# Half-height matmuls on two halves of the array, and weight fetches at spaced times, in a fused attention and mixer kernel

## The chip, the cores and the metric

The kernel runs on one core of one Trainium2 chip. The metric is the device time of one execution in microseconds (us). Most executions of one kernel agree within 0.3%. A core has TensorE (PE, matrix multiplication), VectorE (DVE), ScalarE (ACT), GpSimd (POOL) and SyncE (SP, which here issues all DMAs), each with its own instruction queue that is worked off in order.

## The reference

Batch 4, 8 heads, 576 tokens, head size 64, so a model width of 512. Three stages follow each other:

```python
# 1. attention in a window of 32 (heads 0-3) or 32 dilated by 4 (heads 4-7)
attn = softmax(where(mask, q @ k.T / 8, -1e9)); x = attn @ v            # [4, 576, 512]
# 2. channel mix with token shift
xk, xr = mu_k * x + (1 - mu_k) * x_prev, mu_r * x + (1 - mu_r) * x_prev
x = sigmoid(xr @ w_r) * (relu(xk @ w_k) ** 2 @ w_v)                     # 512 -> 1024 -> 512
# 3. mixer
h = relu(x.T @ w_tok1) @ w_tok2; u = x + h.T                            # 576 -> 256 -> 576 tokens
out = u + relu(u @ w_ch1) @ w_ch2                                       # 512 -> 1536 -> 512
```

All arrays are float32 (weights arrive as 64-bit words and are converted on the core).

## The kernel before

Every large product is made of three matmuls (`mm3`): each operand is split into a high and a low float32r part, and high x high, high x low and low x high are added up in a PSUM bank. A high part is a copy, a low part is the value less the high part (`split`).

The function `tile_model` writes the whole computation down in program order, but nothing is emitted in that order. Each operation goes to a `Plan`, which records its reads and writes and from them its dependencies. `Plan.order` then gives each operation a due time and simulates the five engines: whenever an engine is free, it takes, of the operations that are ready, the one with the smallest due time. What an engine executes is this order. For a matmul the due time begins as the sum of the planned costs of all matmuls ahead of it in the program (`at`); it becomes smaller where something that depends on it is due early:

```python
pad = 0 if first[i] == "tensor" else 1.0
due[i] = min(due[i], due[s] - cost[i] - self.TAIL[first[i]] - self.DELAY[first[i]][first[s]] - pad)
```

`slowly` marks conversions of the channel weights that may be put off: `floor` holds their due times back, and an operation listed there isn't ready before its place `at`.

The stages that the change touches:

**Token mix.** The result of stage 2 lies as 18 tiles of 128 tokens x 512 channels, nine for two batches together: four of batch 0, four of batch 1, and a ninth whose upper 64 rows are the last tokens of batch 0 and whose lower 64 rows are the last tokens of batch 1. `tokens_in(b)` multiplies the four tiles of a batch and the shared one by the first token weights (`t1`, two halves m of 128 hidden units) into two PSUM banks, then rectifies the sums (ACT writes the high part, DVE the remainder) into `hid[b]`. For the shared tile `t1` has two pairs, `t1[4]` with zeros in its lower half and `t1[5]` with zeros in its upper half, so all its matmuls take 128 rows; `ends` keeps the tile's split for the second batch. `turn(t)` transposes a tile into `u`, four PE transposes and their copies. `tokens_out(b)` multiplies `hid[b]` by the second token weights (48 matmuls of 288 columns) in turning banks and adds to `u`. In the trace the first product's matmuls show as `bank<-z,at` (whole tiles), `bank<-wr,at` (shared tile with `t1[4]`, batches 0 and 2) and `bank<-wr,z` (shared tile with `t1[5]`, batches 1 and 3), 512 columns each; those of `tokens_out` as `bank<-at,z`, 288 columns; transposes as `bank<-cst,x`.

**Channel mix.** Both products are done with seven products of half-size blocks in place of eight (names A11, S1, A12, S2, S4, S3, A22), in three column chunks c. The first, `middle(c, j)`, 42 matmuls of 384 columns for each of six j, writes its output through two buffers in turn to DRAM (`kept_mid`, in the trace `part_mid<-at`). The second, `result(c)`, 252 matmuls of 384 columns, loads these back and multiplies by `w2`: seven sweeps, one for each name, 36 matmuls each. The operands of `w2`, seven sets of 6 x 2 x 256 words for each partition, lie in DRAM (`kept_w`, in the trace `part_A..` and `part_S..`) and are fetched into places that the first product's weights `w1` hold until the last `middle` calls; a fetch may be issued as soon as its place is free.

**Attention's last step.** `weigh` multiplies 96 rows x 64 columns, alternately into the upper and lower 64 output partitions, in bursts that the planner keeps together (`burst`). Each float32 matmul shows as two instructions (`bank<-x,at 96*64`). The change doesn't touch it.

Of the kernel before, what the change touches and what calls it, by code (L numbers as in the profile page):

```python
# [10 lines left out]
F32R = mybir.dt.float32r  # L11
# [3 lines left out]
AF = mybir.ActivationFunctionType  # L15
# [134 lines left out]
class Plan:  # L150
# [22 lines left out]
    def __init__(self, nc):  # L173
        self.nc = nc
        self.ops, self.deps, self.ages = [], [], []
        self.state, self.early, self.bursts, self.floor = {}, {}, [], {}
        for name in self.ENGINES:
            setattr(self, name, Plan._Engine(self, name))

# [67 lines left out]
    @staticmethod  # L247
    def _cost(engine, method, kw):

        out = kw["out"]  # L250
        cols = int(np.prod(out.shape[1:]))
        pointers = sum(hasattr(kw.get(k), "space") for k in ("scale", "bias", "scalar", "scalar1"))
        if engine == "sync":
            if kw["in_"].dtype == U32:
                return max(0.45, 4 * cols * out.shape[0] / 230e3 - 0.9)
            return max(0.45, 8 * (0.03 + 4 * cols * 0.0266e-3))
        if engine == "tensor":
            if method == "transpose":
                return cols / 1200 + 0.0025
            if kw["lhsT"].dtype in (F32R, BF16):  # L260
                return cols / 2263 + 0.0049
            if kw["lhsT"].shape[0] <= D or out.shape[0] <= D:
                return cols / 1200 + 0.0025
            return 2 * max(cols / 1200 + 0.0025, 0.112)
        source = kw.get("in_", kw.get("in0"))
        psum = source is not None and "PSUM" in str(source.space)
        if engine == "scalar":
            read = 0.093 * (kw.get("accum_out") is not None)
            return (0.07 if psum else 0.1) + cols / 1200 + 0.03 * pointers + read
        if engine == "gpsimd":  # L270
            return 0.04 if method == "memset" else 0.04 + cols / 345
        if method == "tensor_reduce":
            return 0.066 + int(np.prod(source.shape[1:])) / 960
        if method == "reciprocal":
            return 0.066 + cols / 157
        fast = method in ("tensor_copy", "tensor_scalar", "tensor_scalar_add") and not psum
        return 0.066 + 0.05 * pointers + cols / (1920 if fast else 960)
# [16 lines left out]
    def order(self):  # L294
# [23 lines left out]
            for k, i in enumerate(group[1:]):  # L318
                due[i] = -1e6 + k
        left = [len(d) for d in self.deps]  # L320
        ready = [dict.fromkeys(op, at[i] if i in self.floor else 0.0) for i, op in enumerate(self.ops)]
        known = {e: [] for e in self.ENGINES}
        avail = {e: [] for e in self.ENGINES}
        free = dict.fromkeys(self.ENGINES, 0.6)
# [100 lines left out]
def tile_model(nc, banks, kept_1, kept_w, kept_u, kept_mid, units, cst, mu, w_k, w_v, w_r, w_t1, w_t2, w_c1, w_c2, outT):  # L425
    memory = {k: [Slot(f"{k}{i}", n) for i, n in enumerate(v)] for k, v in SLOTS.items()}

    def f(view):
        return view.bitcast(F32)

    def at(place, shape, dtype=F32):
        name, number, offset = place
        return memory[name][number].view(offset, shape, dtype)
# [6 lines left out]
    def cut(name, numbers, size, count=None):  # L440

        out = []
        for n in numbers:
            out += [(name, n, size * i) for i in range(SLOTS[name][n] // size)]
        return out[:count]
# [7 lines left out]
    def mm3(out, lh, ll, rh, rl, first, last, goes_on=False):  # L453

        more = dict(skip_group_check=True) if goes_on else {}
        nc.tensor.matmul(out=out, lhsT=lh, rhs=rh, start=first, stop=False, **more)
        nc.tensor.matmul(out=out, lhsT=lh, rhs=rl, start=False, stop=False, **more)
        nc.tensor.matmul(out=out, lhsT=ll, rhs=rh, start=False, stop=last, **more)
# [10 lines left out]
    def split(raw, hi, lo):  # L469
        copy(hi, raw)  # L470
        combine(lo, raw, f(hi), ALU.subtract)

    def rows(n):
        return slice(128 * n, 128 * n + 128)
# [6 lines left out]
    def pair(place, shape):  # L481

        name, number, offset = place
        n = int(np.prod(shape))
        return at(place, shape, F32R), at((name, number, offset + n), shape, F32R)
# [11 lines left out]

        return words(w).rearrange("(k p) c -> p k c", p=128)[:, :, 2 * n * m:2 * n * m + 2 * n]

    def single(srcs, t, raw_ring, zero=None):  # L500

        n = t.shape[1]
        flat = raw_ring.tile(2 * n, dtype=U32)
        for part, src in srcs:
            dst = flat[part]
            if len(src.shape) == 3:
                dst = dst.split(src.shape[1], src.shape[2])
            nc.sync.dma_start(out=dst, in_=src)
            if raw_ring is raw_a:
                nc.early[len(nc.ops) - 1] = 6  # L510
        if zero is not None:
            nc.gpsimd.memset(out=f(flat[zero]), constant=0.0)
        raw = flat.split(n, 2)
        low, h = raw[:, :, 0], raw[:, :, 1]
        b, half = t.bitcast(U32), t.bitcast(U16)
        v = nc.vector
        nc.scalar.activation(out=t, in_=f(h), func=AF.Prelu, scale=2.0 ** -112, alpha=-(2.0 ** 32))
        v.tensor_scalar(out=b, in0=b, scalar1=3, scalar2=None, op0=ALU.logical_shift_left)
        v.scalar_tensor_tensor(
            out=half, in0=low, scalar=2.0 ** -29, in1=half, op0=ALU.mult, op1=ALU.add  # L520
        )

    def weight(srcs, hi, lo, raw_ring, tmp_ring, zero=None):

        shape = tuple(hi.shape[1:])
        t = tmp_ring.tile(int(np.prod(shape)))
        single(srcs, t, raw_ring, zero)
        split(t.split(*shape) if len(shape) == 2 else t, hi, lo)

    everything = slice(0, 128)  # L530
# [263 lines left out]
    def slowly(convert, *args):  # L794
        start = len(nc.ops)
        convert(*args)
        nc.floor.update(dict.fromkeys(range(start, len(nc.ops)), SLACK))

    nchunk = len(CHUNKS)
    p_ring = psum(5, 6, 7)  # L800
# [37 lines left out]

    t1 = [pair(p, (HID,)) for p in cut("at", (1, 2), 512) + [("at", 0, 4 * S), ("at", 0, 4 * S + 512), z512[8]]]
    t2 = [pair(p, (S,)) for p in cut("at", (0,), 2 * S, 2)]
    xt512 = cut("xt", (2, 0, 1), 512)
    raw_b, tmp_b = ring(xt512[8:10]), ring(xt512[10:12])
# [1 line left out]
        weight([(everything, words(w_t1)[rows(k), :])], *t1[k], raw_b, tmp_b)  # L846
    tail = words(w_t1)[512:576, :]
    halves = [slice(0, 64), slice(64, 128)]
    for odd in range(2):
        weight([(halves[odd], tail)], *t1[4 + odd], raw_b, tmp_b, zero=halves[1 - odd])  # L850
    for k in range(2):
        for n in range(3):
            cs = slice(192 * n, 192 * n + 192)
# [8 lines left out]

    def u(b, kt, cs):
        return whole[kt // 2][:, kt % 2, S * b:S * b + S][:, cs]

    def tiles_of(b):
        base, odd = 9 * (b // 2), b % 2
        return [(base + 4 * odd + i, i) for i in range(4)] + [(base + 8, 4 + odd)]

    spots = cut("wk", range(4), 512) + cut("xt", (2, 0), 512) + cut("wr", (2,), 512) + cut("x2", (5, 6, 0, 1, 2, 3), 512)  # L870
    w1 = []
# [13 lines left out]

    for j in range(3):
        fetch_1(j)
    hid, ends = {}, {}
    hp_r, x2p_r, up_r = psum(0, 1, 2, 3), psum(4, 5), psum(6, 7)
    late_r = psum(6, 7, 4, 5)  # L890

    def tokens_in(b):
        hp = [hp_r.tile(C) for _ in range(2)]
        for n, (t, kt) in enumerate(tiles_of(b)):
            if n < 4:
                h, l = x2h_r.tile(C, dtype=F32R), x2l_r.tile(C, dtype=F32R)
            elif b % 2 == 0:
                h, l = ends[b // 2] = at(("wr", 3, 0), (C,), F32R), at(("wr", 3, 512), (C,), F32R)
            else:
                h, l = ends[b // 2]  # L900
            if n < 4 or b % 2 == 0:
                split(x2[t], h, l)
            for m in range(2):
                mm3(hp[m], t1[kt][0][:, rows(m)], t1[kt][1][:, rows(m)], h, l, n == 0, n == 4)
        hid[b] = []
        for m in range(2):
            h, l = (hid_r.tile(C, dtype=F32R) for _ in range(2))
            nc.scalar.activation(out=h, in_=hp[m], func=AF.Relu)
            nc.vector.scalar_tensor_tensor(
                out=l, in0=hp[m], scalar=0.0, in1=f(h), op0=ALU.max, op1=ALU.subtract  # L910
            )
            hid[b].append((h, l))

    def turn(t):
        tp = x2p_r.tile(4, 128)
# [13 lines left out]
    def tokens_out(b):  # L929
        for kt in range(4):  # L930
            for n in range(2):
                cs = slice(HALF * n, HALF * n + HALF)
                hp = (up_r if b < 2 else late_r).tile(HALF)
                for k in range(2):
                    h, l = hid[b][k]
                    mm3(hp, h[:, rows(kt)], l[:, rows(kt)], t2[k][0][:, cs], t2[k][1][:, cs], k == 0, k == 1)
                nc.vector.tensor_tensor(out=u(b, kt, cs), in0=hp, in1=u(b, kt, cs), op=ALU.add)
# [5 lines left out]
    for t in range(4, 8):  # L943
        turn(t)
    tokens_in(1)
    tokens_out(0)
    for t in range(9, 13):
        turn(t)
    tokens_in(2)
    turn(17)  # L950
    tokens_out(1)
    for t in range(13, 17):
        turn(t)
    tokens_in(3)
    tokens_out(2)
    tokens_out(3)

# [81 lines left out]
        cut("x2", (1, 2, 3), 512)[2:], cut("wr", (0, 1, 3), 512),  # L1039
    ]  # L1040
    w2 = {}
    for name, places in zip(NAMES, w2_at):
        w2[name] = [tuple(at(p, (2, 256), F32R)[:, i] for i in range(2)) for p in places]
        fetch(places, kept_w[name])

    size = 3 * N2
    half_r = ring(
# [180 lines left out]
```

## Time and profile before

| | |
|---|---|
| time, median of 3 runs (lowest to highest) | 675.2 us (674.82 to 675.28) |
| time of the profiled execution | 676.94 us |
| its span, first to last instruction | 675.2 us |
| PE busy, matmuls | 659.4 us |
| DVE / ACT busy | 547.1 / 332.8 us |
| granted TensorE clock, mean | 1.00 |
| moved by DMA | 138.06 MB, mean 204 GB/s |

A busy engine counts from the first to the last instruction in flight; matmuls overlap, so the step from one start to the next is shorter than one matmul's duration. Times in the rows are us from the span's start.

### The profile page before, as it was taken

The numbers are of one execution on the slowest core, as the hardware profiler recorded it, in microseconds if no ns is written. First come the engines' busy times: TensorE is split into PE (matmuls) and PEld (weight loads), VectorE is DVE, ScalarE is ACT, GpSimd is POOL, SyncE is SP. The second block draws the span as 40 slices with busy tenths as digits, with TensorE's granted clock in tenths as the row PEclk, the third lists the DMA queues.
The fourth block names the chain that finished last, engine by engine and source line by source line (L and its number), as shares of the span: only waits on it lengthen the run. The fifth ranks groups of instructions, "written<-read, shape, count | busy, mean of one in ns | idle before, by whom it ended". The sixth has DMA issues, their size and how long they took to land.

```text
span 675.2 us, 11417 instructions
## 1 busy us (share of the span) xinstructions
PE 659.4 (98%) x4153; PEld 609.8 (90%) x4153; DVE 547.1 (81%) x1127; ACT 332.8 (49%) x886; POOL 2.1 (0%) x22
## 2 busy tenths in 40 slices
PE   6899999999999999999999999999998999999997
PEld 6677888888898888888878999999998999999997
DVE  4899998799689799598877659788695769998982
ACT  4989874578476467375542236563171122212310
POOL 0000000000000000000000000000000000000000
PEclk9999999999999999999999999999999999999999
DMA  8988343556656234428871356947788899632211
GB/s 315 380 318 328 108 145 108 182 160 202 189 169 193 86 138 164 160 79 313 303 252 63 95 205 240 332 174 271 249 298 334 261 390 402 219 94 93 71 36 60
DMA packets 61064, 138.06 MB, mean 204 GB/s; under 512 B 5328, under 2 KB 24656, under 8 KB 59984
## 3 DMA queue, kind: packets, MB, share of 16 engines
q1 hardware_dynamic: 61008, 137.33, 59.4%
q8 instruction: 33, 0.54, 0.3%
q14 instruction: 23, 0.19, 0.1%
HBM read 91.70 MB, written 45.61 MB: 203 GB/s over the span
## 4 chain that ended last, share of the span: by engine, by line
PE 86%; DMA 7%; DVE 3%; ACT 2%; issue 1%; SPq 0%; DVEq 0%; ACTq 0%
PE bank L411 86%; DMA x<-w_k 2%; DMA part_mid<-at 1%; DMA wr<-units 1%; ACT z L411 1%; DVE z L411 1%; DMA wv<-units 1%; DMA raw<-w_v 1%; ACT x L411 1%; DMA xt<-w_t 1%; DVE at L411 1%; DVE xt L411 0%; ACT at L411 0%; SPq L411 0%; DVE x L411 0%
## 5 line engine op out<-in xcount | busy, mean ns | idle before, releaser
L411 PE MATMUL bank<-z,wk 128*128 128x384 f32 x800 | 180.0, 343 | 1.9 <-DVE at L411 1.7
L411 PEld LDWEIGHTS bank<-z,wk 128*128 128x128 f32 x800 | 141.0, 188 | 9.3 <-DVE at L411 2.0
L411 PE MATMUL bank<-wv,z 128*128 128x512 f32 x432 | 129.4, 403 | 0.4 <-ACT z L411 0.4
L411 PEld LDWEIGHTS bank<-wv,z 128*128 128x128 f32 x432 | 78.0, 188 | 12.7 <-ACT z L411 0.8
L411 ACT ACTIVATE at<-at 128x96 f32<-128x96 f32 (+2 forms) x177 | 64.3, 365 | 24.3 <-DVE at L411 22.9
L411 PE MATMUL bank<-wr,z 128*128 128x512 f32 x228 | 62.8, 402 | 1.2 <-DVE z L411 1.2
L411 ACT ACTIVATE z<-bank 128x384 f32<-128x384 f32 (+2 forms) x60 | 29.7, 498 | 52.9 <-PE bank L411 52.6
L411 DVE TENSOR_TENSOR z<-z,z 128x384 fp32r<-128x384 f32 (+1 forms) x94 | 53.0, 569 | 3.1 <-ACT z L411 2.0
L411 PE MATMUL bank<-xt,wk 128*128 128x384 f32 x254 | 53.9, 345 | 1.3 <-ACT at L411 1.3
L411 PEld LDWEIGHTS bank<-wr,z 128*128 128x128 f32 x228 | 41.4, 188 | 8.8 <-DVE z L411 1.6
L411 DVE SCALAR_TENSOR_TENSOR z<-bank,z 128x384 f32<-128x384 f32 (+1 forms) x56 | 31.9, 573 | 21.1 <-ACT z L411 21.1
L411 PE MATMUL bank<-xt,x 128*128 128x384 f32 x248 | 48.8, 334 | 0.0
L411 PE MATMUL bank<-z,x 128*128 128x384 f32 x232 | 47.0, 334 | 0.0
L411 PEld LDWEIGHTS bank<-xt,wk 128*128 128x128 f32 x254 | 44.5, 188 | 2.5 <-issue 1.5
L411 DVE TENSOR_TENSOR at<-bank,at 128x384 f32<-128x384 f32 x64 | 35.3, 552 | 10.7 <-PE bank L411 10.4
L411 PEld LDWEIGHTS bank<-xt,x 128*128 128x128 f32 x248 | 43.5, 188 | 0.0
L411 ACT ACTIVATE z<-z 128x384 fp32r<-128x384 f32 x69 | 35.4, 523 | 11.3 <-DVE z L411 10.0
L411 PEld LDWEIGHTS bank<-z,x 128*128 128x128 f32 x232 | 40.8, 188 | 0.0
L411 ACT ACTIVATE at<-bank 128x384 f32<-128x384 f32 x35 | 17.1, 489 | 38.5 <-PE bank L411 37.6
L411 ACT ACTIVATE x<-bank 96x512 f32<-96x512 f32 (+1 forms) x48 | 28.1, 589 | 14.6 <-PE bank L411 14.3
L411 DVE SCALAR_TENSOR_TENSOR z<-xt,cst,z 128x256 f32<-128x256 f32 (+3 forms) x92 | 34.1, 404 | 0.8 <-ACT z L411 0.4
L411 ACT ACTIVATE z<-xt,cst 128x256 f32<-128x256 f32 (+3 forms) x65 | 26.6, 443 | 10.3 <-DVE z L411 9.9
(170 smaller groups left out, 1164.1 us busy)
## 6 DMA issues: line engine op xcount, KB each, us to landing
part_mid<-at SPq DMA_DIRECT2D x18, 768.0 KB, 5.0
z<-part_mid SPq DMA_DIRECT2D x11, 576.0 KB, 8.0
x<-w_c SPq DMA_DIRECT2D x12, 512.0 KB, 4.0
at<-units SPq DMA_DIRECT2D x14, 416.0 KB, 4.1
unit<-units SPq DMA_DIRECT2D x13, 416.0 KB, 4.4
at<-units SPq DMA_DIRECT2D x21, 256.0 KB, 4.1
part_w<-wv SPq DMA_DIRECT2D x21, 256.0 KB, 3.2
part_w<-x SPq DMA_DIRECT2D x21, 256.0 KB, 3.0
```

Of the source, the lines that this page charges most:

```text
L411: call(kw["out"], kw["constant"]) if method == "memset" else call(**kw)
```

## The change

The fetch of each set of `w2` gets an earliest planned time: the place of the fetches in the plan, plus 5 us for each set ahead of it, less 2 us (`hold`). `floor` and `hold` are told apart: the conversions marked by `slowly` keep both.

The shared tile is no longer padded with zeros. `t1` has one pair for it, whose upper half serves the even batch and whose lower half the odd one. `tokens_in(b)` ends with the four whole tiles, and a new `tokens_end(g)` adds the shared tile for both batches of a group: 64-row matmuls, the even batch on partitions 0 to 63, the odd one on 64 to 127, written down in alternation; then it rectifies all four sums. The planner prices such a matmul at half. Transposes 9 to 12 move ahead of `tokens_out(0)`.

```diff
@@ Plan._cost
             if kw["lhsT"].dtype in (F32R, BF16):
-                return cols / 2263 + 0.0049
+                return (cols / 2263 + 0.0049) * (0.5 if kw["lhsT"].shape[0] <= D else 1)
@@ Plan.order
-        ready = [dict.fromkeys(op, at[i] if i in self.floor else 0.0) for i, op in enumerate(self.ops)]
+        ready = [dict.fromkeys(op, at[i] + self.hold[i] if i in self.hold else 0.0) for i, op in enumerate(self.ops)]
@@ slowly
         nc.floor.update(dict.fromkeys(range(start, len(nc.ops)), SLACK))
+        nc.hold.update(dict.fromkeys(range(start, len(nc.ops)), 0.0))
@@ tile_model, token weights
-    t1 = [pair(p, (HID,)) for p in cut("at", (1, 2), 512) + [("at", 0, 4 * S), ("at", 0, 4 * S + 512), z512[8]]]
+    t1 = [pair(p, (HID,)) for p in cut("at", (1, 2), 512) + [("at", 0, 4 * S), ("at", 0, 4 * S + 512)]]
...
-    for odd in range(2):
-        weight([(halves[odd], tail)], *t1[4 + odd], raw_b, tmp_b, zero=halves[1 - odd])
+    weight([(half, tail) for half in halves], *t1[4], raw_b, tmp_b)
@@ token mix
+    def tokens_end(g):
+        h, l = at(("wr", 3, 0), (C,), F32R), at(("wr", 3, 512), (C,), F32R)
+        split(x2[9 * g + 8], h, l)
+        both = list(zip((2 * g, 2 * g + 1), halves))
         for m in range(2):
...
+            high, low = (w[:, rows(m)] for w in t1[4])
+            for left, right, last in (high, h, False), (high, l, False), (low, h, True):
+                for b, half in both:
+                    nc.tensor.matmul(out=sums_of[b][m], lhsT=left[half], rhs=right[half], start=False, stop=last)
+        for b, _ in both:
+            hid[b] = []
+            for m in range(2):
+                h, l = (hid_r.tile(C, dtype=F32R) for _ in range(2))
+                nc.scalar.activation(out=h, in_=sums_of[b][m], func=AF.Relu)
+                nc.vector.scalar_tensor_tensor(
+                    out=l, in0=sums_of[b][m], scalar=0.0, in1=f(h), op0=ALU.max, op1=ALU.subtract
+                )
+                hid[b].append((h, l))
@@ order of the token mix
     tokens_in(1)
-    tokens_out(0)
+    tokens_end(0)
     for t in range(9, 13):
         turn(t)
+    tokens_out(0)
     tokens_in(2)
     turn(17)
     tokens_out(1)
     for t in range(13, 17):
         turn(t)
     tokens_in(3)
+    tokens_end(1)
     tokens_out(2)
     tokens_out(3)
@@ fetches of w2
-    for name, places in zip(NAMES, w2_at):
+    for n, (name, places) in enumerate(zip(NAMES, w2_at)):
+        start = len(nc.ops)
         w2[name] = [tuple(at(p, (2, 256), F32R)[:, i] for i in range(2)) for p in places]
         fetch(places, kept_w[name])
+        nc.hold.update(dict.fromkeys(range(start, len(nc.ops)), 5.0 * n - 2.0))
```

## Rows read from the trace of the kernel before

**Rows 1.** The page, part 1: busy us, share of the span, instructions

```profile
PE 659.4 (98%) x4153; PEld 609.8 (90%) x4153; DVE 547.1 (81%) x1127; ACT 332.8 (49%) x886; POOL 2.1 (0%) x22
```

**Rows 2.** The chain that ended last, its last part: start us, us, what

```profile
500.07 9.56 DMA part_mid<-at
...
511.23 160.45 PE bank L411 x924
```

**Rows 3.** Timeline of SP's queue, VectorE and PE around 505: start us, us, what

```profile
499.12 0.32 SPq L411 DMA_DIRECT2D wk<-part_A  x1
...
509.75 0.56 DVE L411 TENSOR_TENSOR at<-bank,wr 128x384 f32<-128x384 f32 x1 [3.75 <-DMA part_mid<-at]
...
511.23 1.31 PE L411 MATMUL bank<-z,wk 128*128 128x384 f32 x6 [1.73 <-DVE at L411]
```

**Rows 4.** DMA issues by tile: KB each, median us from issue to landing

```profile
part_mid<-at SPq DMA_DIRECT2D x18, 768.0 KB, 5.0
...
wk<-part_S SPq DMA_DIRECT2D x1, 1024.0 KB, 10.2
```

**Rows 5.** Windows: us, busy of each engine, granted clock, DMA share, GB/s

```profile
440.00:460.00 20.00, 20.00 (x117) 20.00 (x117) 18.22 (x33) 12.82 (x26) 0.00 (x0) 1.00 0.52 178
...
500.00:520.00 20.00, 18.27 (x105) 17.95 (x104) 13.96 (x23) 7.10 (x13) 0.00 (x0) 1.00 0.96 353
...
540.00:550.00 10.00, 10.00 (x60) 10.00 (x59) 4.03 (x6) 0.91 (x2) 0.00 (x0) 1.00 1.04 413
```

**Rows 6.** Timeline of SP's queue, VectorE and PE, 540 to 555

```profile
540.65 1.39 SPq L411 DMA_DIRECT2D z<-part_mid  x2
...
548.72 0.76 DVE L411 CAST wv<-z 128x1152 fp32r<-128x1152 f32 x1 [4.38 <-DMA z<-part_mid]
549.51 2.63 DVE L411 TENSOR_TENSOR wv<-z,wv 128x1152 fp32r<-128x1152 f32 x2
...
554.50 0.68 PE L411 MATMUL bank<-wv,wk 128*128 128x384 f32 x3
```

**Rows 7.** Timeline of PE at the end of the MoE stage

```profile
342.13 3.25 PE L411 MATMUL bank<-wv,z 128*128 128x512 f32 x13 [0.37 <-ACT z L411]
```

**Rows 8.** Timeline of PE: the shared tile's matmuls of batches 0 and 2

```profile
353.99 1.17 PE L411 MATMUL bank<-wr,at 128*128 128x512 f32 x4
...
381.09 1.52 PE L411 MATMUL bank<-wr,at 128*128 128x512 f32 x6
382.45 1.75 PE L411 MATMUL bank<-at,z 128*128 128x288 f32 x12
```

**Rows 9.** Timeline of PE: `tokens_out(0)` beside `tokens_in(1)`

```profile
358.30 0.70 PE L411 MATMUL bank<-at,z 128*128 128x288 f32 x4
358.84 0.39 PE L411 MATMUL bank<-z,at 128*128 128x512 f32 x1
```

**Rows 10.** Timeline of PE: two visits of `weigh`, and a run of scores

```profile
73.18 0.91 PE L411 MATMUL bank<-unit 128*128 128x96 f32 x6
73.87 0.70 PE L411 MATMUL bank<-wv,z 128*128 128x512 f32 x2
...
83.88 0.36 PE L411 MATMUL bank<-at 128*128 128x96 f32 x2
84.02 0.94 PE L411 MATMUL bank<-wv,z 128*128 128x512 f32 x3
84.89 1.15 PE L411 MATMUL bank<-x,at 96*64 96x64 f32 x32
...
86.77 0.27 PE L411 MATMUL bank<-cst,at 128*96 128x128 f32 x1
...
100.22 0.35 PE L411 MATMUL bank<-unit 128*128 128x96 f32 x2
...
101.23 0.69 PE L411 MATMUL bank<-x,at 96*64 96x64 f32 x16
...
102.31 0.36 PE L411 MATMUL bank<-unit 128*128 128x96 f32 x2
```

More of the change, by code (lines that the diff above doesn't have):

```diff
@@ L175, in __init__ @@
         self.ops, self.deps, self.ages = [], [], []
-        self.state, self.early, self.bursts, self.floor = {}, {}, [], {}
+        self.state, self.early, self.bursts, self.floor, self.hold = {}, {}, [], {}, {}
         for name in self.ENGINES:
@@ L498, in col_block, with single @@
         return words(w).rearrange("(k p) c -> p k c", p=128)[:, :, 2 * n * m:2 * n * m + 2 * n]
-    def single(srcs, t, raw_ring, zero=None):
+    def single(srcs, t, raw_ring):
         n = t.shape[1]
@@ L510, in single @@
                 nc.early[len(nc.ops) - 1] = 6
-        if zero is not None:
-            nc.gpsimd.memset(out=f(flat[zero]), constant=0.0)
         raw = flat.split(n, 2)
@@ L521, in single, with weight @@
         )
-    def weight(srcs, hi, lo, raw_ring, tmp_ring, zero=None):
+    def weight(srcs, hi, lo, raw_ring, tmp_ring):
         shape = tuple(hi.shape[1:])
         t = tmp_ring.tile(int(np.prod(shape)))
-        single(srcs, t, raw_ring, zero)
+        single(srcs, t, raw_ring)
         split(t.split(*shape) if len(shape) == 2 else t, hi, lo)
@@ L864, in u @@
         return whole[kt // 2][:, kt % 2, S * b:S * b + S][:, cs]
-    def tiles_of(b):
-        base, odd = 9 * (b // 2), b % 2
-        return [(base + 4 * odd + i, i) for i in range(4)] + [(base + 8, 4 + odd)]
     spots = cut("wk", range(4), 512) + cut("xt", (2, 0), 512) + cut("wr", (2,), 512) + cut("x2", (5, 6, 0, 1, 2, 3), 512)
@@ L887, in tile_model @@
         fetch_1(j)
-    hid, ends = {}, {}
+    hid, sums_of = {}, {}
     hp_r, x2p_r, up_r = psum(0, 1, 2, 3), psum(4, 5), psum(6, 7)
@@ L892, in tokens_in @@
     def tokens_in(b):
[L893 to L902, printed above, removed]
-            for m in range(2):
-                mm3(hp[m], t1[kt][0][:, rows(m)], t1[kt][1][:, rows(m)], h, l, n == 0, n == 4)
-        hid[b] = []
-        for m in range(2):
[L907 to L912, printed above, removed]
+        hp = sums_of[b] = [hp_r.tile(C) for _ in range(2)]
+        for kt in range(4):
+            h, l = x2h_r.tile(C, dtype=F32R), x2l_r.tile(C, dtype=F32R)
+            split(x2[9 * (b // 2) + 4 * (b % 2) + kt], h, l)
+            for m in range(2):
+                mm3(hp[m], t1[kt][0][:, rows(m)], t1[kt][1][:, rows(m)], h, l, kt == 0, False)
+    def tokens_end(g):
+        h, l = at(("wr", 3, 0), (C,), F32R), at(("wr", 3, 512), (C,), F32R)
+        split(x2[9 * g + 8], h, l)
+        both = list(zip((2 * g, 2 * g + 1), halves))
+        for m in range(2):
+            high, low = (w[:, rows(m)] for w in t1[4])
[11 more added lines that the diff above has]
+                hid[b].append((h, l))
     def turn(t):
```

## Prediction

> **What bounds the kernel now.** I read the page first: TensorE (PE) is busy 659.4 of 675.2 us [rows 1], so only what PE executes, or what stops it, can move the end. The granted clock is 1.00 in all stretches [rows 5], so matmuls are priced at one level. The chain of waits came second: behind 511.23 us it is PE alone, 924 matmuls in 160.45 us, 0.174 us for each of 384 columns; ahead of that stands one transfer, a store of `middle`'s output (`part_mid<-at`, 9.56 us) [rows 2]. The last 756 of these matmuls are the three `result` calls (3 x 7 x 36), so these start at 671.68 - 756 x 0.174 = about 540.3 us.
>
> The timeline says what that store did. VectorE sat idle 3.75 us until it had landed, since its buffer of two was the one to be written next, and PE then idled 1.73 us behind VectorE [rows 3]. The usual store lands in 5.0 us [rows 4]. This one shared its transfer time with the fetches of `w2`, which went out as soon as their places were free, from 499.12 us on, over 40 us ahead of some of their uses [rows 3]. The busy windows give the comparison: at the same place of the loop one `c` earlier (440 to 460) the DMA engines were 0.52 busy with 178 GB/s and PE never stopped; at 500 to 520 they were 0.96 busy with 353 GB/s and PE lost 1.73 of 20 us [rows 5].
>
> **Fetches at spaced times.** No transfer is added or removed. `hold` makes fetch n eligible at its place in the plan plus 5n - 2 us. Its place is the sum of the planned matmul time ahead of it. PE lost 15.8 us in all, 3.5 of them after the last matmul (671.68 to 675.2), so 12.3 us before it [rows 1, 2]; the place is near 540.3 - 12.3 = 528 us of trace time, less 2.8 us because the plan now prices the half tiles at half (24 x 0.231 / 2, 0.231 us being the code's price), less 2: A11 near 523 us or a few us before, S1 528, A12 533, S2 538, S4 543, S3 548, A22 553. They are needed at 540.3, 546.6, 552.8, 559.1, 565.4, 571.6, 577.9 (36 x 0.174 = 6.26 us for each sweep). The lead is 17 us or more; the slowest `w2` transfer of the trace landed after 10.2 us [rows 4]. So no sweep waits for its weights, and at 500 us nothing of them is under way. The store then costs 5.0 us, lands near 505 instead of 509.6, which is more than the 3.75 us that VectorE waited, and PE's 1.73 us are gone. Bounds: 0 (the delay was other traffic) and -1.73; I take **-1.73**, by the twin window at 440.
>
> What is late next: fetches moved behind 523 us meet the loads of `part_mid` for the first `result`. VectorE waited 4.38 us for such a load, at 548.72, split it in 0.76 and 2.63 us (to 552.1), and PE used it from 554.50 on [rows 6]. That leaves 2.4 us of cover; of the fetches only S2 stands shortly ahead of that load, so I take 0.
>
> **One conversion fewer.** `t1` loses its sixth pair: the same two DMAs of 128 KB, but one conversion of 256 columns less on ScalarE and VectorE (five instructions) and two GpSimd memsets less. They run beside the last MoE matmuls, where PE's only stop is 0.37 us, behind ScalarE [rows 7]. Bounds 0 and -0.37; I take 0, since PE's cover hides the rest.
>
> **Half tiles.** Before, 24 matmuls of 128 rows x 512 columns, half the rows zero: 12 in each group. Six of them take 381.09 to 382.45, 0.227 us each [rows 8], 5.4 us together. After, 24 matmuls of 64 rows. If each upper half ran beside its lower partner, 12 x 0.227 = 2.7 us would go. For that the two must stand next to each other in PE's order, and this order is not the program's: the planner picks, of what is ready, the smallest due time. The trace shows that: `tokens_out(0)` (288 columns) is mixed into `tokens_in(1)` (512 columns), four against one, although it stands behind it in the code [rows 9].
>
> So I worked out due times from the constants in the code. Call T the planned place at which `tokens_end(0)` begins. Batch 1's half matmuls add to sums which `tokens_in(1)` must have finished: their due times are T to T + 1.3. Batch 0's are due before `tokens_out(0)`. That stands at T + 1.39 + 1.75 (half tiles, then 16 transposes) = T + 3.1, and going back over the remainder (0.60 + 0.08 + 0.20 + 1.0, less 0.27 as the remainder is the third operand), the rectified sum (0.50 + 0.10 + 0.10 + 1.0) and the last matmul (0.2 + 0.12) takes 3.6 us: T - 0.5 at the latest. `tokens_out` turns over two banks only, and each turn costs the due times 2.64 us where PE needs 1.59; three turns and the next user of the banks move this to about T - 4.5. Batch 0's six are ready as soon as `tokens_in(0)` is through, so they go after the first of the four tiles of `tokens_in(1)`, three tiles ahead of batch 1's. Group 1 comes out alike (batch 2 due some 6 us before T, batch 3 just before T). So I expect **no pairs**: 24 matmuls at 0.227 us as before, gain 0.
>
> What is then left is the price of changing the array's partition. No row shows 64 rows x 128 columns. The nearest is `weigh`, 64 output columns on alternate halves of the array, put between full matmuls [rows 10]. The first visit, 83.88 to 86.77, is 2.89 us: two scores (0.115 each, by the six from 73.18 to 73.87), three of 512 columns (0.227), four of 384 (0.174), so 32 small ones and the visit are 2.89 - 0.23 - 0.68 - 0.70 = 1.28. The second, 100.22 to 102.31, with the same but two of 384, is 2.09 - 0.23 - 0.68 - 0.35 = 0.83 for 16 and the visit. The difference gives 0.028 us for a small matmul, and 1.28 - 32 x 0.028 = 0.37 us for a visit. *The Trainium skill, TensorEngine Tiling (Array Packing), Key Properties, says that a change of tiling mode, not of tile, drains TensorE; the trace agrees as far as column halves go, with 0.37 us; the page gives no figure, and no row here shows row halves.*
>
> How many visits: at least 4, one for each batch. Before, batch 0's six stood in runs of 4, 1 and 1 and batch 2's as one run of 6; all four batches together made 3 + 3 + 1 + 2 = 9 runs [rows 8]. By the due times batches 0 and 2 fall between whole-array matmuls due within 0.3 us, so some split; I take 6. Price 6 x 0.37 = **+2.2**, bounds 0 (no drain) and 9 x 0.37 = +3.3.
>
> The rest costs nothing. `tokens_out(0)` waits for batch 0's end as before. Its adds must now follow the copies of transposes 9 to 12, whose cells overlap; 1.8 us of transposes are moved, not added, and PE has other tiles to multiply. Splits and rectifications are the same in number.
>
> **Sum.** -1.73 + 0 + 0 + 2.2 = +0.5 us. The profiled execution took 676.94 us, 1.74 more than its span, and would take 677.4; the median of the runs shown, 675.2, is 1.74 below it, so the forecast is **675.7 us**. A change below 0.2% (1.35 us) can't be told from none.
>
> **Rivals.**
> *B, the visits are free.* Row halves may need no drain. For: a transpose between matmuls costs nothing extra here, so not each change of kind does. Against: the 0.37 us of [rows 10]. Then -1.73, with the conversion -2.1: 673.1 to 673.5.
> *C, the pairs run.* If the planner leaves batch pairs adjacent, 24 take the time of 12: -2.7 - 1.73 + 2 x 0.37 = -3.7: 671.5. Against: the due times. *The Trainium skill, TensorE: Matmul & The Clock Gate, Part 3, says that matmuls on different row groups start about 4 ns apart, and that matmuls keep program order; it gives this gain for neighbours only, and no row here shows it.*
> *D, slower: the spaced fetches delay the loads of the first `result`.* The load issued at 540.65 us landed after 8.1 us; from 10.5 us on PE stops at 554.5 [rows 6]. S4's fetch is 1.57 MB (6 x 2 x 256 words x 128 partitions); if all of it moves ahead of that load, it takes 3.8 us at the 413 GB/s that 540 to 550 reached with the DMA engines full [rows 5], and PE stops for 3.8 - 2.4 = 1.4 us. With the visits that is -1.73 + 1.4 + 2.2 = +1.9: 677.1; if other traffic keeps the stop at 509 as well, up to 678. For: 523 to 553 us gets all 11 MB of `w2`, by itself nearly what the engines move in 30 us at that rate (12.4 MB), and the stores and loads come on top. Against: by the plan the load is issued before S4.
>
> **Chances.** Forecast (no pairs, 4 to 9 visits, no stop: 674.9 to 676.8) 0.42; B 0.25; C 0.07; D 0.22; else 0.04. Range 673.2 to 677.8: it holds B's middle and most of D. Faster: B's greater part and C, 0.28; slower: most of D and the forecast's end above 676.55, 0.3; same 0.42.
>
> **What would show it.** Right: no idle PE near 509; the store of `middle` there lands in about 5 us; `part_A` and `part_S` fetches issued from about 521 us on, 5 us apart; 64-row matmuls in four or more separate runs, batch 0's several us before batch 1's; each run followed or led by about 0.2 to 0.4 us more than its matmuls need. Wrong: 64-row matmuls in alternation with starts under 0.05 us apart (C), or runs that add nothing (B), or a PE stop at 545 to 560 behind a load (D).

## The result and the profile after

The changed kernel took 679.04 us (median of 5 runs, 678.65 to 680.22), the kernel before 675.28 us beside it (5 runs, 674.82 to 676.49). The ratio is 1.0062 with a 95% interval of 1.0051 to 1.0073: slower by 3.4 to 4.9 us. The profiled execution of the kernel after took 679.04 us, its span is 677.3. Forecast were 675.7 us and no difference that can be measured; the time lies above the range as well. Two executions of over 1580 us, one of the kernel before and one of the last experiment, count as slow and are in no median or ratio below.

The page of the kernel after, part 1 (compare [rows 1]): PE is busy 4.5 us longer with the same 4153 instructions.

```profile
PE 663.9 (98%) x4153; PEld 609.4 (90%) x4153; DVE 544.9 (80%) x1121; ACT 334.9 (49%) x887; POOL 1.1 (0%) x20
```

**The fetches.** The timeline of SP's queue, and the busy windows of [rows 5] (us, busy of each engine, granted clock, DMA share, GB/s):

```profile
521.72 1.64 SPq L411 DMA_DIRECT2D wk<-part_A  x2
...
529.01 1.62 SPq L411 DMA_DIRECT2D wk<-part_S  x2
...
534.38 0.42 SPq L411 DMA_DIRECT2D wk<-part_A  x1
```

```profile
440.00:460.00 20.00, 20.00 (x118) 20.00 (x117) 17.50 (x32) 12.44 (x26) 0.00 (x0) 1.00 0.50 182
500.00:520.00 20.00, 20.00 (x118) 20.00 (x117) 16.17 (x25) 9.15 (x16) 0.00 (x0) 1.00 0.56 203
540.00:550.00 10.00, 10.00 (x59) 9.84 (x58) 2.99 (x6) 1.48 (x3) 0.00 (x0) 1.00 1.01 390
```

They are issued from 521.72 us on, as planned. At 500 to 520 the DMA engines are 0.56 busy in place of 0.96, and PE has no gap. At 540 to 550 they are full and PE runs on. The granted clock in these windows stays at 1.00, the upper level. What the spaced fetches delay shows later, at 575 to 583 us; it is taken up under rival D below.

**The half tiles.** The timeline of PE, around batch 0's half tile and around batch 3's (start us, us, matmul, count):

```profile
355.75 1.43 PE L411 MATMUL bank<-wr,at 64*128 64x512 f32 x5
357.11 0.51 PE L411 MATMUL bank<-z,at 128*128 128x512 f32 x1
357.55 0.50 PE L411 MATMUL bank<-wr,at 64*128 64x512 f32 x1
357.98 0.74 PE L411 MATMUL bank<-z,at 128*128 128x512 f32 x2
...
396.30 0.73 PE L411 MATMUL bank<-wr,at 64*128 64x512 f32 x2
396.96 0.50 PE L411 MATMUL bank<-z,at 128*128 128x512 f32 x1
397.38 1.19 PE L411 MATMUL bank<-wr,at 64*128 64x512 f32 x4
```

No half tile stands beside its partner: batch 0's start at 355.75 us, batch 1's at 365.03. The 24 matmuls form ten runs: 2, 3, 3 and 2 in the four batches. One visit can be read off directly. The whole matmul between the fifth and the sixth small one holds PE from 357.11 to 357.55, and the sixth from 357.55 to 357.98: 0.44 and 0.43 us, where a matmul of 512 columns takes 0.227 [rows 8]. So these two changes of height cost 0.42 us.

**The stage as a whole** gives the loss. I measure it from its first transpose to the first matmul of `middle`. The timeline of PE at both ends, kernel after:

```profile
344.21 0.38 PE L411 MATMUL bank<-cst,x 128*128 128x128 f32 x2
...
406.57 0.68 PE L411 MATMUL bank<-z,wk 128*128 128x384 f32 x3
```

The same for the kernel before, in a second profiled execution (taken with the experiments, span 672.7 us):

```profile
344.29 0.38 PE L411 MATMUL bank<-cst,x 128*128 128x128 f32 x2
...
403.00 0.69 PE L411 MATMUL bank<-z,wk 128*128 128x384 f32 x3
```

62.36 us against 58.71: 3.65 us more, 0.365 for each of the ten runs. The first profiled execution of before has 58.72 as well (345.22 to 403.94). In every run of this document the same 362 matmuls stand between the two ends.

### The profile page after: what moved, and what is told of

It reads as the page before. It is cut to its first block, busy times and chain, and to the rows that moved or that the text cites. A ratio compares the mean times of both kernels' runs of the same rounds, so it can differ in the third digit from the quotient of the medians.

```text
span 677.3 us, 11390 instructions
## 1 busy us (share of the span) xinstructions
PE 663.9 (98%) x4153; PEld 609.4 (90%) x4153; DVE 544.9 (80%) x1121; ACT 334.9 (49%) x887; POOL 1.1 (0%) x20
## 4 chain that ended last, share of the span: by engine, by line
PE 85%; DMA 8%; DVE 4%; ACT 1%; issue 0%; SPq 0%; DVEq 0%
PE bank L411 85%; DMA outT<-y 1%; DMA x<-w_k 1%; DMA at<-part_mid 1%; DMA z<-part_mid 1%; DMA wr<-units 1%; DVE z L411 1%; DMA at<-units 1%; DMA wv<-units 1%; DVE x L411 1%; DVE wv L411 1%; ACT z L411 1%; DVE xt L411 1%; DVE at L411 1%; SPq L411 0%
## 5 line engine op out<-in xcount | busy, mean ns | idle before, releaser
L411 PE MATMUL bank<-wr,z 128*128 128x512 f32 x216 | 59.2, 403 | 0.8 <-DVE z L411 0.8
L411 PEld LDWEIGHTS bank<-wr,z 128*128 128x128 f32 x216 | 39.2, 188 | 8.0 <-DVE z L411 1.1
```

The lines of the kernel that those rows point to most:

```text
L411: call(kw["out"], kw["constant"]) if method == "memset" else call(**kw)
```

## The experiments

Theory at the outset (V): the loss is the price of leaving and entering the 64-row mode, about 0.36 us for a run of small matmuls (a visit), ten times; and the stop at 509 us, which the prediction credited with 1.73 us, is not in the usual execution. Rivals: the new order of the stage costs the time (O: waits, not rows); or the spaced fetches do (S).

Each ratio is to runs of the kernel before on the same chip: 675.28 us for the first line, median 674.83 for the next four, 675.64 for the last three. The stage is measured as above; its difference is to 58.71 us.

| kernel | median us | ratio (95%) | stage us | difference | runs of 64 rows |
|---|---|---|---|---|---|
| after | 679.04 | 1.0062 (1.0051 to 1.0073) | 62.36 | +3.65 | 10 |
| spacing alone | 675.6 | 1.0008 (0.9996 to 1.002) | 59.35 | +0.64 | none |
| half tiles alone | 679.84 | 1.0065 (1.0049 to 1.0082) | 62.34 | +3.63 | 10 |
| before, 64 rows in its own order | 679.18 | 1.0059 (1.0042 to 1.0075) | 62.05 | +3.34 | 9 |
| after, halves bound in pairs | 674.04 | 0.9987 (0.9977 to 0.9997) | 56.49 | -2.22 | 2 |
| the same, fetches not spaced | 672.65 | 0.9956 (0.9938 to 0.9973) | 56.49 | -2.22 | 2 |
| halves bound, one after the other | 674.69 | 0.9985 (0.9971 to 0.9999) | 57.45 | -1.26 | 2 |
| one bound run for each batch | 681.01 | 1.0075 (1.0049 to 1.0102) | 59.98 | +1.27 | 4 |

The +0.64 of spacing alone, with no 64-row matmul in it, is one stop of PE behind VectorE at 349.77 us (0.38 us idle by the profile). So a difference of some tenths of a us in this column says little.

### The kernel before once more

> The kernel before once more. If PE's stop of 1.73 us near 509 belongs to every execution, it is there again and the span is near 675. Theory: VectorE's wait for the store is there, shorter, PE doesn't stop there, and the span is near 673.5.

674.43 us, span 672.7. The timeline of VectorE, and the window at 500:

```profile
507.24 0.56 DVE L411 TENSOR_TENSOR at<-bank,wr 128x384 f32<-128x384 f32 x1 [2.11 <-DMA part_mid<-at]
```

```profile
500.00:520.00 20.00, 19.90 (x115) 19.58 (x114) 14.82 (x24) 6.72 (x12) 0.00 (x0) 1.00 0.94 357
```

The fetches go out as early as in [rows 3], the DMA engines are as busy (0.94, 357 GB/s), and VectorE waits for the same store, 2.11 us in place of 3.75. PE has no stop behind VectorE there; it loses 0.10 of 20 us, not 1.73. So PE's cover behind that store, the time by which VectorE may be late before PE stops, is about 2 us (2.11 - 0.10; in [rows 3] 3.75 - 1.73), and the stop of [rows 3] is what one execution showed beyond it.

### Spacing alone

```diff
# before, with only these edits of the change, and the two other lines that `hold` needs
+        nc.hold.update(dict.fromkeys(range(start, len(nc.ops)), 5.0 * n - 2.0))
-        ready = [dict.fromkeys(op, at[i] if i in self.floor else 0.0) for i, op in enumerate(self.ops)]
+        ready = [dict.fromkeys(op, at[i] + self.hold[i] if i in self.hold else 0.0) for i, op in enumerate(self.ops)]
```

> The kernel before with the fetches of w2 held back as in the change, the shared tile as before. Theory V (the visits of 64-row matmuls make the loss): no loss here; PE's stop of 1.73 us near 509 is gone from the profile, so 0 to -1.7 us against the median before, nearer 0 if that stop is not in every execution. Rival S (the spaced fetches make the loss by crowding the loads of the first result): +1 to +3 us, with PE stops between 545 and 600.

The window at 500 to 520 of this kernel:

```profile
500.00:520.00 20.00, 20.00 (x117) 20.00 (x116) 15.39 (x24) 7.22 (x13) 0.00 (x0) 1.00 0.45 155
```

The spacing does empty the DMA engines (0.45), and the time doesn't fall: 0.3 us less to 1.4 us more. A gain of 1.73 us in the median is excluded.

### Half tiles alone

The kernel after, without the `hold` line of the `w2` fetches.

> The changed kernel with the w2 fetches issued as early as before. Theory V: the whole loss stays, +3.5 to +4 us in the token mix (ten visits of 0.4 us), and a stop near 509 may come back. Rival S: the loss is gone, within 1 us of before.

The window of this kernel, fuller than that of [rows 5] (1.01, 380 GB/s), and VectorE's wait for the store:

```profile
500.00:520.00 20.00, 20.00 (x117) 19.82 (x116) 15.83 (x25) 9.32 (x15) 0.00 (x0) 1.00 1.01 380
```

```profile
511.25 0.56 DVE L411 TENSOR_TENSOR at<-bank,wr 128x384 f32<-128x384 f32 x1 [1.88 <-DMA part_mid<-at]
```

PE doesn't stop. The whole loss is there without the spacing, which leaves the half tiles.

### 64 rows, in the order of before

```diff
# before: tokens_in, t1[4] and t1[5] padded with zeros as they were
+            part = halves[b % 2] if n == 4 else everything
             for m in range(2):
-                mm3(hp[m], t1[kt][0][:, rows(m)], t1[kt][1][:, rows(m)], h, l, n == 0, n == 4)
+                lh, ll = (w[part][:, rows(m)] for w in t1[kt])
+                mm3(hp[m], lh, ll, h[part], l[part], n == 0, n == 4)
```

Only the shared tile's 24 matmuls change, from 128 rows to 64; every engine keeps the order of before.

> The kernel before with nothing changed but the rows: the shared tile's 24 matmuls read 64 of the 128 rows (t1 keeps both pairs, planned prices and order stay). Nine runs of such matmuls, as before. Theory V: 9 x 0.4 = +3.6 us, all of it between 350 and 400. Rival O (the loss comes from the new order of the token mix, not from the row halves): 0.

The timeline of PE, to be held against [rows 8]:

```profile
354.43 1.19 PE L411 MATMUL bank<-wr,at 64*128 64x512 f32 x4
355.55 0.33 PE L411 MATMUL bank<-cst,x 128*128 128x128 f32 x1
355.81 0.49 PE L411 MATMUL bank<-wr,at 64*128 64x512 f32 x1
...
383.02 0.61 PE L411 MATMUL bank<-z,at 128*128 128x512 f32 x2
383.57 1.66 PE L411 MATMUL bank<-wr,at 64*128 64x512 f32 x6
385.15 1.86 PE L411 MATMUL bank<-at,z 128*128 128x288 f32 x12
```

The six of batch 2 take 1.58 us to the next start (383.57 to 385.15), where the same six took 1.36 with 128 rows, and the twelve behind them show 1.86 in place of 1.75 [rows 8]: 0.22 + 0.11 = 0.33 us. The two whole matmuls ahead of them take 0.55 us to the next start (383.02 to 383.57) in place of 2 x 0.227 = 0.45, which makes it about 0.42 us for one visit, as in the one read off above. Nine runs cost the stage 3.34 us, 0.37 each. The order is out of the question as a cause: the matmuls of the whole kernel stand in the same order as before, and the stage loses nearly what it loses in the changed kernel (3.34 and 3.65 us).

### The halves bound in pairs

```diff
# tokens_end, kernel after
+        start = len(nc.ops)
         for m in range(2):
...
+        nc.burst(start)
```

`burst` keeps the twelve matmuls of a group together, in the written order, so that each upper half stands beside its lower partner.

> The changed kernel with the twelve half matmuls of a group bound together (the planner's burst), so each upper one stands next to its lower partner: two visits in place of ten. Theory V with pairs running side by side: matmul time 24 x 0.227 = 5.4 becomes 2.7, visits 2 x 0.4 = 0.8: -1.9 us against before in the token mix. If neighbours don't overlap: 5.4 + 0.8: +0.8 us. Rival O: PE stops behind the rectified sums of all four batches, +2 us or more.

The timeline of PE, group 0:

```profile
357.92 2.09 PE L411 MATMUL bank<-z,at 128*128 128x512 f32 x8
359.94 1.66 PE L411 MATMUL bank<-wr,at 64*128 64x512 f32 x12
361.53 1.09 PE L411 MATMUL bank<-cst,x 128*128 128x128 f32 x8
```

Twelve matmuls in 1.59 us, where one after the other they would need 12 x 0.227 = 2.7. In the trace the partners of this group start 3 to 4 ns apart (2 to 10 in the other group) and the pairs about 0.23 us, after a first step of 0.34, as if one half were free. So what the change was built for works as soon as the order lets it.

### Pairs bound, fetches as early as before

The kernel above without the `hold` line of the `w2` fetches.

> The kernel of e4 (pairs bound together) with the w2 fetches issued as early as before. Theory V: the pairs make the whole gain, two visits of about 0.4 us less 2.7 us of matmul time, -2 us; the spacing is worth nothing in the median, so the same as e4 within 0.7 us, -0.5 to -2. Rival S2 (the spacing costs half a us, as the median of e1 hints): about 0.5 us faster than e4. Rival S3 (the spacing makes e4's gain): 675 or more.

The timelines of VectorE and of PE, their only stops near 509:

```profile
505.06 0.56 DVE L411 TENSOR_TENSOR at<-bank,wr 128x384 f32<-128x384 f32 x1 [2.27 <-DMA part_mid<-at]
```

```profile
506.53 1.31 PE L411 MATMUL bank<-z,wk 128*128 128x384 f32 x6 [0.26 <-DVE at L411]
```

672.65 us: faster than both kernels, by 1.8 to 4.2 us against before. VectorE's wait of 2.27 us reaches PE with 0.26, which puts the cover behind the store at about 2.0 us in this kernel as well.

### The halves bound, one after the other

```diff
# tokens_end: the upper half's six first, then the lower half's six, in one burst
-        for m in range(2):
-            high, low = (w[:, rows(m)] for w in t1[4])
-            for left, right, last in (high, h, False), (high, l, False), (low, h, True):
-                for b, half in both:
+        for b, half in both:
+            for m in range(2):
+                high, low = (w[:, rows(m)] for w in t1[4])
+                for left, right, last in (high, h, False), (high, l, False), (low, h, True):
```

> The kernel of e4, but in each burst the six matmuls of the upper half come first, then the six of the lower half: two visits still, the same matmuls, only no alternation. If only neighbours on different halves overlap: 12 x 0.227 = 2.7 us a group in place of 1.4, so +2.7 us against e4, about 676.5. Rival (the visit alone decides, and halves overlap in any order or not at all): the same as e4.

The timeline of PE, group 0, and the twelve starts in the trace, in us from the first:

```profile
361.29 2.22 PE L411 MATMUL bank<-wr,at 64*128 64x512 f32 x12
363.45 0.77 PE L411 MATMUL bank<-cst,x 128*128 128x128 f32 x5
```

```
upper half   0      0.335  0.570         0.803         1.039         1.263
lower half                        0.576         0.911         1.146         1.375  1.607  1.838
```

The trace doesn't name the halves; I read the starts as two streams because each then shows the steps of a bound run: 0.335 first, then 0.23. In program order the upper half's fourth matmul would have started 6 ns after its third, which no other run shows within one half. Twelve matmuls take 2.16 us, between the 1.59 of the pairs and 2.7 one by one. My expectation had them one by one and was too dear: the lower half's first starts beside the upper half's third, ahead of three that stand before it in the program.

### One bound run for each batch

As above, but a `burst` for each batch: four visits, no partners.

> The changed kernel with one burst for each batch: six matmuls of 64 rows together, four visits, no pairs. Theory V: 24 x 0.227 = 5.4 us as before plus 4 x 0.4 = 1.6: +1.6 us against before, 2.4 us less than the change with its ten visits: about 676.5. Rival O (the order of the stage, not the number of visits): +4 as the change.

The timeline of PE, batch 0's run, and the stop ahead of the stage:

```profile
343.93 3.40 PE L411 MATMUL bank<-wv,z 128*128 128x512 f32 x13 [2.83 <-ACT z L411]
...
358.70 1.65 PE L411 MATMUL bank<-wr,at 64*128 64x512 f32 x6
360.29 1.66 PE L411 MATMUL bank<-z,at 128*128 128x512 f32 x6
```

The stage is as expected: 1.27 us for four visits, 0.32 each. The total isn't. This plan has a stop of 2.83 us at the end of the channel mix of stage 2 (the MoE stage of [rows 7]), which was 0.42 in the second execution of before. The timeline of ScalarE shows its beginning:

```profile
343.09 0.37 ACT L411 ACTIVATE xt<-xt 128x192 f32<-128x192 f32 x1 [4.22 <-DMA xt<-w_t]
343.36 0.51 ACT L411 ACTIVATE z<-z 128x384 fp32r<-128x384 f32 x1
```

ScalarE waits 4.22 us for a load of the token weights with the conversion that PE needs right behind it in its queue; in before it waits 0.93 there. Each edit re-plans that place, so comparisons of whole times carry it as noise of the plan: PE's stop behind ScalarE at that place was 0.89 us in the 64-row kernel and 1.28 in the one-after-the-other kernel. The stop and the visits make up most of the profiled execution's loss (679.2 us); the median is 1.8 us above that one, and why stays open.

## Why the prediction was wrong

**The stop at 509, -1.73 us: this step failed.** "By the twin window at 440" I gave the whole stop to the fetches' traffic. Traffic does lengthen VectorE's wait; but in four of five executions with early fetches and full DMA engines (0.90 to 1.02 busy: before once more, half tiles alone, 64 rows, pairs with early fetches) PE lost 0 to 0.26 us there. [Rows 3] had a warning beside them: the profiled execution took 676.94 us, 1.74 more than the median, the size of the stop. By setting the sum against the profiled execution and then taking 1.74 off to reach the median, I in effect took the same stop off twice. That the two sizes agree is in part chance: the first profiled execution's span is 2.5 us above the second's, and 0.93 of that arose ahead of the stage (345.22 against 344.29). The term for the median run is 0, and the spacing alone measured +0.5 us (-0.3 to +1.4).

**The visits, +2.2 us: right price, wrong count.** 0.37 us from `weigh`'s column halves [rows 10] (the sum as written gives 0.38); row halves measured 0.365 in the kernel after, 0.37 in the order of before and 0.32 in the four bound runs. The trace agrees with *the Trainium skill, TensorEngine Tiling (Array Packing), Key Properties*, that a change of tiling mode drains TensorE, now for row halves too. I took six runs with a bound of nine (+3.3 us); there were ten, +3.65 us. This step failed too. The due times decide how often a run is broken up, and the order of before already gave nine.

Together: 675.2 + 3.65 = 678.9 us against 679.04 measured. The two steps are 1.73 + 1.45 = 3.18 of the 3.34 us missed. That so little is left over is in part luck: the spaced fetches cost some tenths of a us too (rival D below).

**No pairs: right,** and by the reason given: batch 0's halves came 9.3 us before batch 1's. Rival C needed only this: bound in pairs the kernel has the stage 2.22 us shorter, where twelve matmuls saved (2.72 us) and two visits at 0.37 (0.74) would give 1.98. Its 671.5 us wasn't reached, as it counted the stop's 1.73 us too.

**Rival B, free visits: wrong.** The 64-row kernel in the order of before excludes it. **The conversion, 0: right** within what the place shows; PE's stop of 0.37 us [rows 7] is gone after, but it varies with each plan.

**Rival D: its wait is there, its stop stands elsewhere.** VectorE waited 4.71 us for `z<-part_mid` at 549.82, later than [rows 6] by 1.1 us, and PE used the split at 555.28 without a gap. But the last two sets go out at 554.66 to 558.11 us, and stores of the first `result` land later. VectorE and PE in the kernel after:

```profile
575.30 0.56 DVE L411 TENSOR_TENSOR z<-bank,z 128x384 f32<-128x384 f32 x1 [1.53 <-DMA outT<-z]
...
578.44 0.55 DVE L411 TENSOR_TENSOR z<-bank,z 128x384 f32<-128x384 f32 x1
...
579.09 4.12 PE L411 MATMUL bank<-xt,wr 128*128 128x384 f32 x20 [0.25 <-issue]
...
581.99 0.56 DVE L411 TENSOR_TENSOR y<-bank,z 128x384 f32<-128x384 f32 x1 [0.93 <-DMA outT<-y]
```

The window 570 to 600 of the kernel after, of half tiles alone, and of the bound pairs with and without spacing, in this order:

```profile
570.00:600.00 30.00, 29.61 (x169) 29.00 (x169) 25.64 (x27) 8.20 (x7) 0.00 (x0) 1.00 0.85 322
570.00:600.00 30.00, 29.91 (x173) 29.59 (x172) 28.76 (x31) 8.20 (x7) 0.00 (x0) 1.00 0.66 231
570.00:600.00 30.00, 29.54 (x170) 28.92 (x169) 27.16 (x29) 7.67 (x7) 0.00 (x0) 1.00 0.75 275
570.00:600.00 30.00, 30.00 (x175) 30.00 (x174) 29.00 (x31) 8.20 (x7) 0.00 (x0) 1.00 0.53 172
```

VectorE waits 1.53 us for an output store; in half tiles alone the same operation, at 575.31, waits for nothing. So VectorE has read PE's bank only at 578.99, and PE's last sweep of this `result`, which by the code goes on in that bank, begins 0.1 us behind. The profile names no releaser there; I read the cause from these times. So the spacing moved a stop rather than removing it. From the first `z,wk` matmul to the end of the last matmul the three pairs of kernels that differ by the spacing alone took, with and without it, 266.8 and 266.2 us (after, half tiles alone), 267.1 and 266.5 (bound pairs), 266.3 and 266.1 (spacing alone, before once more): 0.1 to 0.6 us more with it, of one execution each.

**Open.** What the spacing costs in the median: alone +0.5 us (-0.3 to +1.4), and the bound pairs came to 0.9987 with it and 0.9956 without, against different runs of before on one chip; but half tiles alone, without it, were no faster than the kernel after (679.84 and 679.04 us). Why one execution has the long store and others not was not tried.

## What to carry to other kernels

A matmul of fewer rows is no cheaper by itself: unless its partner runs beside it, it takes the columns' time and pays for each change of height, so count these changes in the order that is emitted, and bind the partners together. Before the removal of a stall is credited, look whether the profiled execution stands above the median by that stall's size, and profile a second one. Where a planner re-sorts everything, measure the stage that changed by itself, since other stages move too (here 0 to 2.8 us at one place), and look past the place that a transfer was moved from to where it now runs.

## What the runs showed of the hardware

- Matmuls of 64 rows by 128 columns cost 0.32 to 0.37 us for each run of them between whole ones (0.42 in the one read off directly); inside a run they take 0.23 us for 512 columns, like 128 rows.
- Upper and lower half run fully beside each other: pairs of 512 columns start about every 0.23 us, the two of a pair 3 to 4 ns apart in one group and 2 to 10 in the other. This agrees with the start distance of about 4 ns in *the Trainium skill, TensorE: Matmul & The Clock Gate, Part 3*.
- The halves needn't alternate in the program: twelve matmuls, one half after the other, took 0.56 us less than 2.72. As I read the starts above, as two streams, a matmul for the free half started ahead of three earlier ones for the busy half. The same Part 3 says that matmuls start in program order; the starts, read so, differ from that.
